# Attention with a spectral mix: the last sixteen modes regrouped by row transfers

## The chip, the cores and the metric

The kernel runs on one core of one Trainium2 chip. The metric is the device time of one execution in microseconds (us), lower is better. Of several runs the median is taken.

## The reference

The first half is a linear attention over 8 batches, 8 heads, 576 positions and 64 features per head. The second half mixes its result `x` (8 x 576 x 512) in the frequency domain: of the Fourier transform along the positions, the first 64 modes are multiplied by a complex 512 x 512 matrix each, transformed back and added, and a dense layer with a relu follows.

```python
X = np.fft.rfft(x, axis=1)
Xr, Xi = (np.real(X[:, :n_modes]), np.imag(X[:, :n_modes]))          # n_modes = 64
Yr = np.einsum('bmd,mde->bme', Xr, w_r) - np.einsum('bmd,mde->bme', Xi, w_i)
Yi = np.einsum('bmd,mde->bme', Xr, w_i) + np.einsum('bmd,mde->bme', Xi, w_r)
Y[:, :n_modes] = Yr + 1j * Yi
y = np.fft.irfft(Y, n=S, axis=1)
u = x + y
return (u + np.maximum(u @ w_ch, 0.0)).astype(np.float32)
```

## The kernel before

**The modes.** The 64 mode matrices come in 32 steps, `k` = 0 to 31. A step from k=8 on takes a group `gi` of eight modes (0 to 7) and 128 of the 512 input features, and loads two weight tiles, real (`wr`) and imaginary (`wi`), with one DMA each from the POOL queue (L162); `NW` = 3 steps may be in flight. `mode_mm` (L416) makes eight products with `wr` and eight with `wi` into one PSUM tile `psY`; each fills 32 of its 128 rows. For the last eight steps (k=24 to 31) the sum over the feature blocks is complete after the step: `mode_sum` (L444, VectorE) adds `psY` to the accumulator and leaves `yst`, which has a row for each mode, part (real or imaginary) and batch; the batch is the row's number modulo 8. Steps k=30 and k=31 are the groups gi=6 and gi=7, the last sixteen modes.

**From modes to batches.** The output needs the spectrum by batch: the tile `zy` has 128 rows (modes and parts) by [Z or Y, batch, 512], where Y is the spectrum and Z is Y times `w_ch`. `yst` is transposed on TensorE (L805), copied to `sY` by VectorE (L806), and for each pair of groups `by_batch` makes, in two halves h of four batches, Z (`mm_z`, L705) and Y itself (`mm_r`, a product with the identity, L711), 32 rows at a time, because a product takes the 32 columns of one batch from `sY`. The results lie in two PSUM tiles `psZY` (tags T0 and T1). For the first three pairs they are copied to `zy` by ScalarE (h=0) and VectorE (h=1), L718, a bit at a time, out of a list `copies` that `pieces` works off. For the last pair one batch of each half is copied in place (batches 0 and 4), and the whole of `psZY` is copied to `st` (L735), from which six DMAs of 64 KB, two on SP and four on POOL, move the other rows (L737).

**The work beside it.** `pieces` also runs the products of `x` with `w_ch` ahead: `flip_x` transposes a pair of tiles of `xs_all` (TensorE L654 into PSUM tag T3, VectorE copy `sT` L657), and `times_w` multiplies them (L665 into `psW`, tag T2, ScalarE copy `xw` L667). `reordered` (L692, `psX`, tags T0 and T1; copy L694) permutes rows of `xs_all`. Every PSUM tag has one buffer, so a tile waits until the tag's last tile has been read.

**The output units.** Twenty units, five for each pair of batches (b, b+4), in the order (b, b, b+4, b+4, both). A unit adds `xw` through an identity (`add_xw`, L753) and the transform of Z (`add_z`, L760) in a tile `psB`, relu by ScalarE (L762); `x` (`add_x`, L768) and the transform of Y (`spec`, L774) in `psA`, added by VectorE (L776). "Late" units add `x` on GpSimd (L780) instead. The result leaves by DMA from SP (L856). For unit 0 (`u0`), `add_xw` and `add_x` are run early, within k=31; its `psB` has tag T2 and its `psA` tag T3.

**Order.** All of this runs under a manual schedule: each engine runs its instructions in the order of the program text, and waits where data or a buffer is not ready. In step k=30 the end of the text is `times_w`; step k=31 begins with `add_xw(u0)`, then `mode_mm`, `mode_sum` in two halves, the transposes in two halves (T0, T1), `add_x(u0)`, `by_batch`.

Of the kernel before, what the change touches and what calls it, by code (L numbers as in the profile page):

```python
# [10 lines left out]
F32 = mybir.dt.float32  # L11
F32R = mybir.dt.float32r
BF16 = mybir.dt.bfloat16
I32 = mybir.dt.int32
ACT = mybir.ActivationFunctionType
ALU = mybir.AluOpType
# [4 lines left out]
DMODEL = 512  # L21
# [5 lines left out]
def kernel(  # L27
# [11 lines left out]
    nc = tc.nc  # L39
# [4 lines left out]
    psum = psum_cm.__enter__()  # L44
    pw = ctx.enter_context(tc.tile_pool(name="pw", bufs=3))

    ident_b = const.tile([128, 128], BF16, name="ident_b")
# [8 lines left out]
    Yacc = pers.tile([128, 8, DMODEL], F32, name="Yacc")  # L56
    wchb = pers.tile([128, 4, DMODEL], BF16, name="wchb")
# [54 lines left out]
    W = {}  # L112
# [274 lines left out]
                             start=(dc == 0), stop=(dc == 3))  # L387
        nc.scalar.copy(xw0[:, i, :], ps)

    def mode_mm(k, tag="yr"):  # L390
        g, gi = groups[k]
        XT = XTs[1 - g if k < 8 else g % 2]
        wt = W.pop(k)
        if gi < 0:
            psY = psum.tile([128, 2, DMODEL], F32, name="psY2", tag="pC", bufs=1)
            for par in range(2):
                for ri in range(2):
                    for j in range(4):
                        for x in range(2):
                            r = slice(64 * x, 64 * x + 64)  # L400
                            m = 16 * (-1 - gi) + 8 * x + 2 * j + par
                            c0 = (16, 0, 48, 32)[2 * ri + par]
                            nc.tensor.matmul(
                                psY[32 * j:32 * j + 32, x, :],
                                lhsT=XT[r, c0:c0 + 32, m],
                                rhs=wt[ri][r, 2 * j + par, :],
                                start=(par == 0 and ri == 0), stop=(par == 1 and ri == 1),
                            )
            return psY
        psY = psum.tile([128, DMODEL], F32, name="psY", tag=tag, bufs=1)  # L410
        for ri in range(2):
            for par in range(2):
                for j in range(4):
                    m = 8 * gi + 2 * j + par
                    c0 = (16, 0, 48, 32)[2 * ri + par]
                    nc.tensor.matmul(  # L416
                        psY[32 * j:32 * j + 32, :],
                        lhsT=XT[:, c0:c0 + 32, m],
                        rhs=wt[ri][:, 2 * j + par, :],
                        start=(par == 0 and ri == 0), stop=(par == 1 and ri == 1),  # L420
                    )
        return psY

    def mode_sum(k, psY, pb=None):
        g, gi = groups[k]
        if gi < 0:
            G = -1 - gi
            if g == 0:
                nc.vector.tensor_copy(Yacc[:, 2 * G:2 * G + 2, :], psY)
            else:  # L430
                nc.vector.tensor_tensor(
                    out=Yacc[:, 2 * G:2 * G + 2, :], in0=psY, in1=Yacc[:, 2 * G:2 * G + 2, :],
                    op=ALU.add)
        elif g < 3:
            nc.vector.tensor_tensor(  # L435
                out=Yacc[:, gi, :], in0=psY, in1=Yacc[:, gi, :], op=ALU.add)
        else:

            cuts = [0, DMODEL] if k < 31 else [0, DMODEL // 2, DMODEL]
            yst = []  # L440
            for a, b in zip(cuts, cuts[1:]):
                t = pb.tile([128, b - a], BF16, name="yst", tag="yst" if k < 31 else f"yst{a}",
                            bufs=2 if k < 31 else 1)
                nc.vector.tensor_tensor(out=t, in0=psY[:, a:b], in1=Yacc[:, gi, a:b], op=ALU.add)  # L444
                yst += [t[:, x:x + 128] for x in range(0, b - a, 128)]
            return yst


# [76 lines left out]
    psY = None  # L525
# [3 lines left out]
    with tc.manual_schedule():  # L529
# [25 lines left out]
        for n in range(N + 2):  # L555
# [9 lines left out]
            if psY is not None:  # L565
                mode_sum(k_out, psY)
                psY = None
# [54 lines left out]
            if k_out < K_IN_ATTN and n >= after[k_out] + 2:  # L622
                psY = mode_mm(k_out)
# [10 lines left out]
    pb = ctx.enter_context(tc.tile_pool(name="pb", bufs=2))  # L634

    psum = ctx.enter_context(tc.tile_pool(name="psumT", bufs=1, space=bass.MemoryType.PSUM))
# [4 lines left out]
    zy = pb.tile([128, 2, B_, DMODEL], BF16, name="zy", bufs=1)  # L641
    zall, yall = zy[:, 0], zy[:, 1]
# [5 lines left out]
    copies = []  # L648
# [11 lines left out]
    def times_w():  # L660
        i, sT = ahead.pop(0)
        ps = psum.tile([128, 2, DMODEL], F32, name="psW", tag="T2")
        for x in range(2):
            for dc in range(4):
                nc.tensor.matmul(ps[:, x, :], lhsT=sT[:, x, dc, :], rhs=wchb[:, dc, :],  # L665
                                 start=(dc == 0), stop=(dc == 3))
        nc.scalar.copy(xw[:, i - N_EARLY:i + 2 - N_EARLY, :], ps)  # L667
# [29 lines left out]
    def by_batch(sY, P):  # L697
        cols = [sY[:, dc].rearrange("p g c -> p (g c)") for dc in range(4)]

        ps = [psum.tile([128, 2, DMODEL], F32, name="psZY", tag=f"T{h}") for h in range(2)]  # L700

        def mm_z(h):
            for dc in range(4):
                for j in range(4):
                    nc.tensor.matmul(ps[h][32 * j:32 * j + 32, 0, :], lhsT=cols[dc][:, j + 4 * h::8],  # L705
                                     rhs=wchb[:, dc, :], start=(dc == 0), stop=(dc == 3))

        def mm_r(h):
            for dc in range(4):
                for j in range(4):  # L710
                    nc.tensor.matmul(  # L711
                        ps[h][32 * j:32 * j + 32, 1, dc * 128:(dc + 1) * 128],
                        lhsT=cols[dc][:, j + 4 * h::8], rhs=ident_b, start=True, stop=True)

        rows = slice(32 * P, 32 * P + 32)

        def copy(j, h, eng):
            eng(zy[rows, :, j + 4 * h, :], ps[h][32 * j:32 * j + 32])  # L718

        if P < 3:  # L720
            for h in range(2):
                mm_z(h)
                mm_r(h)
            copies.extend([lambda j=j: (copy(j, 0, nc.scalar.copy),
                                        copy(j, 1, nc.vector.tensor_copy)) for j in range(4)])
            return

        for h, eng in ((0, nc.scalar.copy), (1, nc.vector.tensor_copy)):  # L730
            mm_z(h)
            mm_r(h)
            copy(0, h, eng)
            st = pb.tile([128, 2, DMODEL], BF16, name=f"st{h}", bufs=1)
            eng(st, ps[h])  # L735
            for j in range(1, 4):
                (nc.sync if j == 1 else nc.gpsimd).dma_start(  # L737
                    zy[rows, :, j + 4 * h, :], st[32 * j:32 * j + 32])

    def parts(u):
# [21 lines left out]
    def add_x(u):  # L764
        u["psA"] = ps = psum.tile([128, 2, DMODEL], F32, name="psA", tag=u["tags"][1])
        if not u["late"]:
            for r, x, b, c, idn, ci in parts(u):
                nc.tensor.matmul(ps[r, x, :], lhsT=idn, rhs=xs_all[:, b * NCH + c, :],  # L768
                                 start=True, stop=False)
# [15 lines left out]
    with tc.manual_schedule():  # L785
        plan = {22: 3, 23: 3, 24: 2, 25: 2, 26: 2, 27: 1, 28: 2, 29: 1, 30: 1, 31: 0}
        while k_out < 32:
            k = k_out
            gi = groups[k][1]
            while k_in < min(k_out + NW, 32):  # L790
                weights(k_in)
                k_in += 1
            if k == 31:
                add_xw(u0)
            yst = mode_sum(k, mode_mm(k, "T3"), pb)
            k_out += 1
            if yst is not None:
                if ahead:
                    times_w()
                if gi % 2 == 0:  # L800
                    sY = pb.tile([128, 4, 2, 128], BF16, name="sY", tag="sY")
                for a, b, tag in ((0, 4, "T3"),) if k < 31 else ((0, 2, "T0"), (2, 4, "T1")):
                    pt = psum.tile([128, b - a, 128], BF16, name="ptY", tag=tag)
                    for dc in range(a, b):
                        nc.tensor.transpose(pt[:, dc - a, :], yst[dc], ident_b)  # L805
                    nc.vector.tensor_copy(sY[:, a:b, gi % 2, :], pt)  # L806
                if k == 31:
                    add_x(u0)
                if gi % 2 == 1:
                    by_batch(sY, gi // 2)  # L810
            pieces(plan[k])
            if k <= 24 or k % 2 == 0:
                assert not copies
                for tag in ("T0", "T1"):
                    if reorder:
                        reordered(tag)
            if k == 30:
                times_w()
        assert not todo and not ahead and not reorder and not copies

    units = []
# [65 lines left out]
```

## Time and profile before

| | before |
|---|---|
| median of 3 runs | 456.16 us (455.45 to 456.48) |
| profiled execution, first to last instruction (its span) | 456.7 us; the profile gives no other time of its own |
| TensorE busy | 301.7 us (66%) |
| VectorE busy | 292.0 us (64%) |
| ScalarE busy | 261.8 us (57%) |
| GpSimd busy | 198.8 us (44%) |
| DMA | 97.70 MB, 214 GB/s on average |
| mean granted TensorE clock | 0.883 of full speed |

A row of the profile's timeline has the start and duration in us, the engine (PE is TensorE, PEld its weight load, DVE VectorE, ACT ScalarE, POOL GpSimd, SP the sync engine), the line of the kernel, the operation, what it writes and reads, the shape, how many such instructions were merged, and in brackets how long the engine was idle before it and what ended that. The granted clock is the share of full speed at which TensorE may run. Busy shares are means over stages that differ: the weights stream in until shortly before the end, and the last 40 us are the output.

### The profile page before, as it was taken

How to read it: one execution, taken by the hardware profiler on the slowest of the kernel's cores; microseconds unless marked ns; L12 is line 12 of the kernel's file. 1: busy time of each engine (PE TensorE's matmuls, PEld its weight loads, DVE VectorE, ACT ScalarE, POOL GpSimd, SP SyncE). 2: the span in 40 equal slices, each digit the busy share in tenths (PEclk: the TensorE clock that was granted, in tenths of full speed). 3: DMA queues.
4: the chain of work that ended last, by engine and by line, in shares of the span. 5: the costliest groups of instructions: out<-in, count | busy, mean ns of one | idle time of the engine just before them, and what ended most of it. 6: DMA issues, size and time to landing. Idle time of an engine off the chain costs nothing.

```text
span 456.7 us, 11065 instructions
## 1 busy us (share of the span) xinstructions
PE 301.7 (66%) x4637; PEld 197.6 (43%) x4637; DVE 292.0 (64%) x418; ACT 261.8 (57%) x528; POOL 198.8 (44%) x251
## 2 busy tenths in 40 slices
PE   3476776833767677655555544755578878868993
PEld 2355565622555565544333432433344445433341
DVE  6578789844988779876666472776322273653873
ACT  4576887833686877865545452765334455644662
POOL 3956476445563256553435231443021212100993
PEclk9976899876886769998778595999999999998997
DMA  6999999999999999999999999999999999990697
GB/s 179 195 228 222 225 213 226 221 206 216 221 228 217 230 219 222 224 219 229 218 207 217 218 218 218 207 203 207 207 207 207 207 207 207 207 179 11 223 341 299
DMA packets 84417, 97.70 MB, mean 214 GB/s; under 512 B 3152, under 2 KB 77136, under 8 KB 84368
## 3 DMA queue, kind: packets, MB, share of 16 engines
q0 software_dynamic: 75728, 76.75, 101.1%
q1 hardware_dynamic: 8480, 20.19, 12.8%
q8 instruction: 36, 0.59, 0.5%
q14 instruction: 13, 0.11, 0.1%
q10 hardware_dynamic: 160, 0.07, 0.1%
HBM read 163.64 MB, written 9.44 MB: 379 GB/s over the span
## 4 chain that ended last, share of the span: by engine, by line
DMA 34%; issue 24%; DVE 17%; PE 11%; POOL 7%; ACT 3%; SPq 1%; DVEq 0%; POOLq 0%; ACTq 0%
DMA wi<-in_moe_w_i_dram 29%; DVE mkq L233 6%; DMA wr<-in_moe_w_r_dram 4%; DVE xs_all L336 2%; DVE nd L322 2%; DVE tB L315 2%; POOL vaug L270 2%; PE ptr L184 1%; PE psNB L305 1%; ACT AA L240 1%; PE kvz L286 1%; PE psB L753 1%; DVE of L776 1%; SPq L122 1%; POOL wr L162 1%
## 5 line engine op out<-in xcount | busy, mean ns | idle before, releaser
L270 POOL TENSOR_TENSOR vaug<-vn,ee 128x576 bf16<-128x576 f32 x64 | 72.7, 1155 | 63.3 <-ACT ee L255 50.2
L240 ACT ACTIVATE AA<-psT 128x1024 bf16<-128x1024 f32 x64 | 62.0, 1021 | 43.6 <-PE psT L208 43.1
L262 ACT ACTIVATE e<-mkq 64x4 f32<-64x4 f32 (+1 forms) x128 | 26.3, 206 | 61.5 <-DVE mkq L233 59.2
L244 ACT ACTIVATE AA<-psk 128x1024 bf16<-128x1024 f32 x64 | 61.4, 1010 | 0.0
L162 POOL DMA_DIRECT2D wr<-in_moe_w_r_dram x24 | 21.9, 912 | 86.6 <-PE psY L416 77.8
L416 PEld LDWEIGHTS <-XT 128*32 128x32 bf16 x384 | 17.1, 171 | 56.6 <-issue 46.4
L667 ACT CAST xw<-psW 128x1024 bf16<-128x1024 f32 x17 | 17.2, 1013 | 40.5 <-PE psW L665 34.6
L233 DVE TENSOR_REDUCE mkq<-psk 128x8 f32<-128x1024 f32 x32 | 38.8, 1213 | 0.7 <-PE psk L199 0.7
L233 DVE TENSOR_REDUCE mkq<-psq 128x8 f32<-128x1024 f32 x32 | 38.9, 1217 | 0.4 <-PE psq L199 0.4
L435 DVE TENSOR_TENSOR Yacc<-psY,Yacc 128x512 f32<-128x512 f32 x16 | 11.0, 689 | 42.5 <-PE psY L416 42.5
L416 PE MATMUL psY<-wi,XT 128*32 128x512 bf16 x192 | 18.0, 435 | 28.8 <-DMA wi<-in_moe_w_i_dram 28.8
L286 PE MATMUL kvz<-vaug,AA 64*128 64x65 bf16 x1152 | 29.2, 210 | 11.5 <-POOL vaug L275 9.8
L190 DVE COPY kT<-ptr 128x640 bf16<-128x640 bf16 x32 | 15.7, 492 | 32.5 <-PE ptr L184 32.5
L665 PE MATMUL psW<-wchb,sT 128*128 128x512 bf16 x136 | 33.5, 391 | 2.1 <-ACT xw L667 2.1
L315 DVE TENSOR_TENSOR tB<-psNB,e 128x650 f32<-128x650 f32 x32 | 26.7, 833 | 11.2 <-PE psNB L305 10.6
L305 PEld LDWEIGHTS <-AA 128*128 128x128 bf16 x640 | 29.0, 110 | 9.3 <-issue 8.9
L286 PEld LDWEIGHTS <-AA 64*128 64x128 bf16 x1152 | 25.1, 107 | 15.9 <-issue 11.8
L162 POOL DMA_DIRECT2D wi<-in_moe_w_i_dram x24 | 21.1, 880 | 23.8 <-PE psY L416 20.5
L322 DVE TENSOR_TENSOR nd<-psNA,tB 128x650 f32<-128x650 f32 x32 | 26.7, 835 | 4.1 <-DVE tB L315 0.5
L416 PE MATMUL psY<-wr,XT 128*32 128x512 bf16 x192 | 17.0, 424 | 18.0 <-DMA wr<-in_moe_w_r_dram 8.7
L336 DVE TENSOR_TENSOR xs_all<-nd,rden 128x640 bf16<-128x640 f32 x32 | 28.0, 874 | 1.1
L184 PE MATMUL ptr<-ident_b,k 128*128 128x128 bf16 x160 | 17.9, 257 | 14.8 <-DVE qT L190 12.6
(132 smaller groups left out, 705.4 us busy)
## 6 DMA issues: line engine op xcount, KB each, us to landing
wr<-in_moe_w_r_dram POOLq DMA_DIRECT2D x24, 1024.0 KB, 25.8
wi<-in_moe_w_i_dram POOLq DMA_DIRECT2D x24, 1024.0 KB, 29.4
wr<-in_moe_w_r_dram POOLq DMA_DIRECT2D x16, 512.0 KB, 15.9
wi<-in_moe_w_i_dram POOLq DMA_DIRECT2D x16, 512.0 KB, 19.6
out_dram<-of SPq DMA_DIRECT2D x16, 512.0 KB, 3.8
vn<-in_v_dram SPq DMA_DIRECT2D x24, 288.0 KB, 5.8
q<-in_q_dram POOLq DMA_DIRECT2D x12, 288.0 KB, 19.3
k<-in_k_dram POOLq DMA_DIRECT2D x12, 288.0 KB, 20.0
```

What stands on the lines that cost most here:

```text
L162: nc.gpsimd.dma_start(t, w[8 * gi:8 * gi + 8, g * 128:(g + 1) * 128, :].rearrange("m p e -> p m e"))
L233: nc.vector.tensor_reduce(out=o, in_=i, axis=AX.X, op=ALU.max, apply_absolute_value=True)
L240: nc.scalar.activation(AA[:, 0, ab, 0:1024].rearrange("f (x j p) -> f j x p", j=2, p=64), st["psT"].rearrange("f j (x p) -> f j x p", p=64 ...
L244: nc.scalar.activation(AA[:, 1, ab, 0:1024].rearrange("p (c j f) -> p j c f", c=4, j=2), st["psk"], ACT.Exp, scale=sc)
L270: nc.gpsimd.tensor_tensor(out=vaug[:, ab, :, 0:64], in0=st["v"], in1=ee[:, ab, :].unsqueeze(2).to_broadcast([128, 9, D_]), op=ALU.mult,)
L286: nc.tensor.matmul(kvz[:, hh, ab * 65:(ab + 1) * 65], lhsT=AA[r, 1, ab, 128 * j:128 * j + 128], rhs=vaug[r, ab, j, :], start=(j == 0), sto ...
L305: nc.tensor.matmul(p[:, hh, 65 * c:65 * c + 65], lhsT=AA[:, 0, ab, x:x + 128], rhs=kvzF[:, hh, ab * 65:(ab + 1) * 65], start=True, stop=True,)
L315: nc.vector.tensor_tensor(out=tB, in0=st["psNB"], in1=e2.unsqueeze(3).to_broadcast([128, 2, NCH, 65]), op=ALU.mult,)
L322: nc.vector.tensor_tensor(out=nd, in0=st["psNA"], in1=st["tB"], op=ALU.add)
L336: nc.vector.tensor_tensor(out=xo, in0=nd[:, :, :, 0:64], in1=rden.to_broadcast([128, 2, NCH, 64]), op=ALU.mult,)
L416: nc.tensor.matmul(psY[32 * j:32 * j + 32, :], lhsT=XT[:, c0:c0 + 32, m], rhs=wt[ri][:, 2 * j + par, :], start=(par == 0 and ri == 0), sto ...
L665: nc.tensor.matmul(ps[:, x, :], lhsT=sT[:, x, dc, :], rhs=wchb[:, dc, :], start=(dc == 0), stop=(dc == 3))
```

## The change

Groups gi=6 and gi=7 no longer go through `by_batch`. For each, `by_row` moves the rows of `yst` to `yall` by seven DMAs of 16 rows (16 KB), one for each batch from 1 to 7: batches 4 and 1 on SP, 5, 2, 6, 3, 7 on POOL. `z_of_group` makes Z of the group as one product of 128 rows (four matmuls of 128 x 512 into `psZ`: tag T3 for group 6, T1 for group 7), copies it half by ScalarE and half by VectorE to `z8`, and moves the rows by the same seven DMAs to `zall`. So there are 28 transfers of 16 KB where there were 6 of 64 KB. Batch 0 of both groups is made in place (`first_batch`, tag T0): four Z products and four identity products of 32 rows, copied to `zy` by ScalarE and VectorE. Batch 4, which was copied in place, comes by DMA.

In step k=31 the real products of `mode_mm` come first and lie in tag T1 (T3 before); then `times_w` (which was the end of step 30) and `add_x(u0)`, then the imaginary products, then `add_xw(u0)` (which was the first of the step). `yst` has one tile with three buffers.

```diff
-    def mode_mm(k, tag="yr"):
+    def mode_mm(k, tag="yr", ris=(0, 1), psY=None):
...
-        psY = psum.tile([128, DMODEL], F32, name="psY", tag=tag, bufs=1)
-        for ri in range(2):
+        if psY is None:
+            psY = psum.tile([128, DMODEL], F32, name="psY", tag=tag, bufs=1)
+        for ri in ris:
...
+            yst = pb.tile([128, DMODEL], BF16, name="yst", tag="yst", bufs=3)
             cuts = [0, DMODEL] if k < 31 else [0, DMODEL // 2, DMODEL]
...
-        for h, eng in ((0, nc.scalar.copy), (1, nc.vector.tensor_copy)):
+        for h in range(2):
             mm_z(h)
             mm_r(h)
-            copy(0, h, eng)
-            st = pb.tile([128, 2, DMODEL], BF16, name=f"st{h}", bufs=1)
-            eng(st, ps[h])
-            for j in range(1, 4):
-                (nc.sync if j == 1 else nc.gpsimd).dma_start(
-                    zy[rows, :, j + 4 * h, :], st[32 * j:32 * j + 32])
-
+        copies.extend([lambda j=j: (copy(j, 0, nc.scalar.copy),
+                                    copy(j, 1, nc.vector.tensor_copy)) for j in range(4)])
+
+    def by_row(all_b, t, gi):
+        for b in (4, 1, 5, 2, 6, 3, 7):
+            (nc.sync if b in (4, 1) else nc.gpsimd).dma_start(
+                all_b[16 * gi:16 * gi + 16, b, :], t[b::8, :])
+
+    def first_batch(sY):
+        cols = [sY[:, dc].rearrange("p g c -> p (g c)")[:, 0::8] for dc in range(4)]
+        ps = psum.tile([128, 2, DMODEL], F32, name="psZY", tag="T0")
+        r = slice(96, 128)
+        for dc in range(4):
+            nc.tensor.matmul(ps[r, 0, :], lhsT=cols[dc], rhs=wchb[:, dc, :],
+                             start=(dc == 0), stop=(dc == 3))
+        for dc in range(4):
+            nc.tensor.matmul(ps[r, 1, dc * 128:(dc + 1) * 128], lhsT=cols[dc], rhs=ident_b,
+                             start=True, stop=True)
+        nc.scalar.copy(zall[r, 0, :], ps[r, 0, :])
+        nc.vector.tensor_copy(yall[r, 0, :], ps[r, 1, :])
+
+    def z_of_group(sY, gi):
+        ps = psum.tile([128, DMODEL], F32, name="psZ", tag="T3" if gi == 6 else "T1")
+        for dc in range(4):
+            nc.tensor.matmul(ps, lhsT=sY[:, dc, gi % 2, :], rhs=wchb[:, dc, :],
+                             start=(dc == 0), stop=(dc == 3))
+        z = pb.tile([128, DMODEL], BF16, name="z8", tag="z8")
+        nc.scalar.copy(z[:, 0:256], ps[:, 0:256])
+        nc.vector.tensor_copy(z[:, 256:512], ps[:, 256:512])
+        by_row(zall, z, gi)
...
-            if k == 31:
+            if k < 31:
+                psY = mode_mm(k, "T3")
+            else:
+                psY = mode_mm(k, "T1", ris=(0,))
+                times_w()
+                add_x(u0)
+                mode_mm(k, ris=(1,), psY=psY)
                 add_xw(u0)
-            yst = mode_sum(k, mode_mm(k, "T3"), pb)
+            yst = mode_sum(k, psY, pb)
             k_out += 1
             if yst is not None:
+                if gi >= 6:
+                    by_row(yall, yst, gi)
                 if ahead:
                     times_w()
...
-                if k == 31:
-                    add_x(u0)
-                if gi % 2 == 1:
+                if gi == 7:
+                    first_batch(sY)
+                if gi >= 6:
+                    z_of_group(sY, gi)
+                elif gi % 2 == 1:
                     by_batch(sY, gi // 2)
             pieces(plan[k])
...
-            if k == 30:
-                times_w()
```

More of the change, by code (lines that the diff above doesn't have):

```diff
@@ L388, in times_w_early @@
         nc.scalar.copy(xw0[:, i, :], ps)
-    def mode_mm(k, tag="yr"):
+    def mode_mm(k, tag="yr", ris=(0, 1), psY=None):
         g, gi = groups[k]
         XT = XTs[1 - g if k < 8 else g % 2]
-        wt = W.pop(k)
+        wt = W[k]
         if gi < 0:
@@ L437, in mode_sum @@
         else:
+            yst = pb.tile([128, DMODEL], BF16, name="yst", tag="yst", bufs=3)
             cuts = [0, DMODEL] if k < 31 else [0, DMODEL // 2, DMODEL]
-            yst = []
             for a, b in zip(cuts, cuts[1:]):
[L442 to L445, printed above, removed]
+                nc.vector.tensor_tensor(out=yst[:, a:b], in0=psY[:, a:b], in1=Yacc[:, gi, a:b],
+                                        op=ALU.add)
             return yst
@@ L718, in copy @@
             eng(zy[rows, :, j + 4 * h, :], ps[h][32 * j:32 * j + 32])
[L720 to L726, printed above, removed]
-        for h, eng in ((0, nc.scalar.copy), (1, nc.vector.tensor_copy)):
+        for h in range(2):
             mm_z(h)
             mm_r(h)
-            copy(0, h, eng)
-            st = pb.tile([128, 2, DMODEL], BF16, name=f"st{h}", bufs=1)
-            eng(st, ps[h])
-            for j in range(1, 4):
-                (nc.sync if j == 1 else nc.gpsimd).dma_start(
-                    zy[rows, :, j + 4 * h, :], st[32 * j:32 * j + 32])
+        copies.extend([lambda j=j: (copy(j, 0, nc.scalar.copy),
[25 more added lines that the diff above has]
+        by_row(zall, z, gi)
     def parts(u):
@@ L804 @@
                     for dc in range(a, b):
-                        nc.tensor.transpose(pt[:, dc - a, :], yst[dc], ident_b)
+                        nc.tensor.transpose(pt[:, dc - a, :], yst[:, dc * 128:(dc + 1) * 128],
+                                            ident_b)
                     nc.vector.tensor_copy(sY[:, a:b, gi % 2, :], pt)
-                if k == 31:
-                    add_x(u0)
-                if gi % 2 == 1:
+                if gi == 7:
[3 more added lines that the diff above has]
+                elif gi % 2 == 1:
                     by_batch(sY, gi // 2)
```

## The prediction

> **What bounds the kernel now.** I read the page first, then the timeline from 400 us to the end, the granted clock in steps of 1 us from 404 to 421, the landing of the last weights, and the DMA issues after 395 us. Until the weights of the last group (k=31) have landed the kernel waits for the weight stream: the page's chain gives 29% of the span to the imaginary weights. Behind that landing there is a serial piece, and then the output units, which TensorE, GpSimd and the output DMA all but fill. The change lies in the piece between.
>
> The last weight issue and its landing: 388.44 + 26.0 = 414.4 us (the issue of k=30, at 380.99, is the one that took 23.6: its products start on the landing).
>
> ```profile
> 388.44 0.88 POOL L162 DMA_DIRECT2D wi<-in_moe_w_i_dram  x1
> ...
> DMA to landing us min/median/max: 23.6/24.8/26.0
> ```
>
> The timeline from k=30 to the first outputs (start, duration, what; in brackets idle time and who ended it):
>
> ```profile
> 407.42 0.42 DVE L806 COPY sY<-ptY 128x512 bf16<-128x512 bf16 x1 [1.36 <-PE ptY L805]
> 407.90 0.61 PE L654 MATMUL pt<-ident_b,xs_all 128*128 128x128 bf16 x8 [0.52 <-DVE sY L806]
> 408.54 0.69 DVE L657 COPY sT<-pt 128x1024 bf16<-128x1024 bf16 x1 [0.70 <-PE pt L654]
> 409.26 2.46 DVE L718 CAST zy<-psZY 32x1024 bf16<-32x1024 f32 x2
> 410.29 0.59 PE L692 MATMUL psX<-xs_all,ident_p 128*128 128x512 bf16 x2 [1.79 <-ACT zy L718]
> 410.72 3.22 PE L665 MATMUL psW<-wchb,sT 128*128 128x512 bf16 x8
> 413.98 1.01 ACT L667 CAST xw<-psW 128x1024 bf16<-128x1024 f32 x1 [2.05 <-PE psW L665]
> 415.04 0.59 PE L753 MATMUL psB<-xw,ident_p 128*128 128x512 bf16 x2 [1.10 <-ACT xw L667]
> 415.56 0.69 PE L416 MATMUL psY<-wr,XT 128*32 128x512 bf16 x8
> 416.08 0.60 PE L416 MATMUL psY<-wi,XT 128*32 128x512 bf16 x8
> 417.55 0.62 DVE L806 COPY sY<-ptY 128x256 bf16<-128x256 bf16 x2
> 421.93 1.23 DVE L735 CAST st<-psZY 128x1024 bf16<-128x1024 f32 x1
> 423.07 2.35 DVE L776 TENSOR_TENSOR of<-psA,of 128x1024 f32<-128x1024 f32 x2
> 425.50 8.40 POOL L780 TENSOR_TENSOR of<-of,xs_all 128x1024 f32<-128x1024 f32 x4 [0.98 <-DVE of L776]
> 425.77 2.52 DVE L776 TENSOR_TENSOR of<-psA,of 128x1024 f32<-128x1024 f32 x2 [0.36 <-ACT of L762]
> ```
>
> Two facts decide. The imaginary products of k=31 start at 416.08, 1.6 us after their weights: they stand behind psW, its ACT copy and psB. And psW took 3.22 us here, where the same eight products take 1.89 to 1.90 at 392.54 and 405.26. The windows say why (PE, PEld, DVE, ACT, POOL, then clock, DMA share, GB/s):
>
> ```profile
> 409.00:410.00 1.00, 0.00 (x0) 0.00 (x0) 0.97 (x2) 0.99 (x2) 0.00 (x0) 1.00 0.64 108
> 411.00:412.00 1.00, 1.00 (x4) 0.34 (x3) 0.73 (x1) 0.93 (x1) 0.00 (x0) 0.56 0.38 62
> 412.00:413.00 1.00, 1.00 (x4) 0.42 (x3) 0.00 (x0) 0.00 (x0) 0.00 (x0) 0.50 0.17 28
> ```
>
> After a thin stretch (of the 3.4 us before 411.1 TensorE was busy 1.4: the transposes' 0.61 and 0.8 from 410.29) the clock is half for 3.4 us; that stretch was then dense and full speed returned at 414.5.
>
> **The change, part by part.** Times are those of this execution, 456.66 us from first to last instruction, 0.50 above the median of 456.16.
>
> *k=30.* Group 6 gets its Z product between the sY copy (ends 407.84) and flip_x, in the same PSUM tag T3. Four products 128x512: 1.03 us, as the four psX products at 378.16. ACT copies 256 columns: 1024 take 1.01 and 512 take 0.60 (relu into Yacc), so 0.40 by the slope. DVE's half waits for ACT's (the built program's wait list has it): 0.38, as one half of the two yst adds (0.76). With hand-overs of 0.05: 1.95. flip_x waits for that DVE copy to free T3, so its transposes go from 407.90 to 409.86, sT to 410.50, the two DVE copies out of psZY from 409.26–411.72 to 411.22–413.68. psX, which waits for ACT's copies, goes from 410.29 to about 411.5. The row transfers of group 6 (5 on POOL and 2 on SP for each of Y and Z) queue behind the last weights and delay nothing that is awaited; POOL has no other work then. They add 0.22 MB to a stream of 207 GB/s: at most 1.1 us on the landing, which has more than that to spare below.
>
> *k=31, real products first.* psY now lies in T1, and T1 holds psZY of the previous pair until DVE's second copy ends, 413.68. So the real products start at 413.74, not early. Behind them in TensorE's order: times_w (8 products), add_x (2), then the imaginary products. At full clock 0.43 + 1.72 + 0.43 from 413.74 gives 416.3. At half clock a 512-column product takes 0.43 (the weight loads of psW stand at 411.60, 412.03, 412.45, 412.88): 0.86 + 3.43 + 0.43 to 0.86. What was done while the weights came is now done after them.
>
> *Which clock?* From 408.97 (end of the Z products) to 413.74 TensorE has only the transposes (0.61) and psX (0.59) in 4.8 us. A stretch like 407.7–411.1 holds 1.6 of 3.4, and 411.1–414.5 some 1.4: as thin as the 1.4 that brought half clock before. I take half clock until 417.9, then full: real products to 414.6, times_w to 418.03, add_x to 418.46, imaginary products done 419.06 against 416.68. add_xw waits for ACT's copy of psW (418.2 + 1.01), ends 419.7, and the transposes behind it start there, 0.2 later than yst allows. The second sY copy ends at 420.67 against 418.17: 2.50 late.
>
> The Trainium skill ("TensorE: Matmul & The Clock Gate", Part 1) has it that the clock halves after an idle window of about 3.4 us, and asks for no idle gaps above that; by that the full clock would hold here, since the longest gap is 1.7 us, and the time is that of the first rival below. The trace does not agree: half clock came at 411.1 with no gap above 1.8 us (408.51 to 410.29). The same page's Part 4 says that transposes don't count as busy, which would make the stretch thinner still; no run here shows that alone.
>
> *After sY.* Before: 64 products (418.20–420.64), then on ACT 1.00 + 1.01 and on DVE 1.22 + 1.23 (copy, st); unit 0's add at 423.07, unit 2's at 425.77, that is 4.90 and 7.60 after sY. Now the first batch's four Z products (0.86, the first two already on the first half of sY) and four small ones (0.22) end at 421.65. ACT copies 32x512 (0.60), DVE after it 0.67 (half of 1.22 and a fixed part). The group's Z product ends 422.5, ACT's half of it 422.95, then relu of unit 0 to 424.03, its add at 424.07; unit 1's add 425.65–426.88. Unit 2 (batch 4) used to be copied in place and now needs the z8 transfer: issued on SP behind z8's DVE half, 423.45, and 2.1 to land (the zy<-st issues on SP): 425.55. Then two Z products 0.60, relu 1.02, and the add at 427.3, or 6.6 after sY against 7.6. Gain 0.97. SP's four transfers stand ahead of the first output but cost it nothing (it is ready at 425.3). POOL issues five more, 423.45 + 5 x 0.56 = 426.3, before its first add, which needs unit 1 at 426.9 (425.50 before, 1.4 late). From there the units run as before: TensorE is busy 4.9 to 5.0 of 5 us, POOL idles 0.8 us between 425.50 and 449.45.
>
> Sum: 2.50 – 0.97 = 1.5 by unit 2, 1.4 by POOL. I take 1.45: 458.1 in a profiled execution, 457.6 in the median. The boundary of the clock's stretch can lie elsewhere: half clock ending 417.1 gives 420.2 for sY (+1.0), ending 419.2 gives 421.15 (+2.0). So 457.2 to 458.1 for this case.
>
> **The rivals.**
> 1. *Full clock through.* Real products to 414.2, times_w to 415.9, imaginary products done 416.95, add_xw from 417.2, sY 418.6: 0.43 late, minus 0.97, is –0.55: 455.6, not slower. For: several stretches about 0.5 busy kept full clock (the late slices of the page show 9 throughout). Against: the row at 411. It decides if the stretch before 414.5 counts as busier than the one before 411.1.
> 2. *The imaginary products do start on the landing* (414.5) at full clock, because DVE's copies leave T1 some 2 us earlier than I have it and times_w is through by then: done 415.1, sY 416.7, –1.5 – 0.97 = –2.5: 453.7. For: that is how the order is written. Against: T1's copies stand behind sT, sT behind the Z product.
> 3. *POOL decides.* If a row transfer costs POOL the 0.88 of a weight issue and not 0.56, five from 423.45 end at 427.85, 1.0 after unit 1's add; POOL has no slack, so +2.5: 458.6. It decides above 0.69 each. Against: the 64 KB issues took 0.54 to 0.56, and these are smaller.
>
> **How the numbers follow.** Forecast 0.60, rivals 0.20, 0.08 and 0.12. 0.2% (0.9 us) is about what a measurement of this kernel can tell. Faster: rival 2 and a fifth of rival 1 (a tail gain above mine), 0.12. Same: the rest of rival 1, and 0.08 for the low end of the forecast, whose 457.2 is next to the bound: 0.24. Slower: 0.64. The range runs from rival 1 to the long half clock with a little of rival 3, 455.5 to 458.9; the forecast's own is 457.0 to 458.4.
>
> **What would show it.** In the changed profile: the real products of k=31 starting near 413.7, released by DVE's zy copy; psW behind them taking 3.2 to 3.4; imaginary products starting near 418.4, over 3 us after the landing; unit 0's add some 3.4 after sY; unit 2's Z products released by a DMA. Wrong if the real products start before 412, if the clock stays 1.00 from 411 to 418, or if POOL's first add waits for POOL itself.

## The result

The changed kernel is slower: 459.41 us in the median of 22 runs (458.06 to 461.21), against 456.98 for the kernel before, run beside it 22 times (455.39 to 460.27). The ratio is 1.005, with a 95% interval of 1.0033 to 1.0066, that is +2.4 us. The forecast was 457.6 with a range to 458.9: the direction came, the size did not, and the time lies above the range. Of the 1.8 us between forecast and time, 0.8 is the base (a median of 456.16 in three runs, 456.98 in 22); the other 1.0 is the change itself, which was forecast at +1.45. The profiled execution has a span of 458.7 us at a mean clock of 0.867, and the time measured for it is 460.56. In all 22 runs the time is 1.73 to 1.86 us longer than the span (on record to 0.1 us), a figure that was not known when the forecast was made, and that matters below.

The last weights of the changed kernel are issued at 390.5 and land 22.4 us later, at 412.9:

```profile
L162 POOL DMA_DIRECT2D wi<-in_moe_w_i_dram x1: 881/881/881, 390.5 to 390.5; - x1
...
DMA to landing us min/median/max: 18.2/20.3/22.4
```

The timeline of the changed kernel from step 30 to the first units (start, duration, engine, line, operation, what it writes and reads; in brackets the idle time and who ended it):

```profile
408.42 0.42 DVE L827 COPY sY<-ptY 128x512 bf16<-128x512 bf16 x1 [0.49 <-PE ptY L825]
410.37 0.42 DVE L750 CAST z<-psZ 128x256 bf16<-128x256 f32 x1 [1.53 <-ACT z L749]
410.85 0.61 PE L653 MATMUL pt<-ident_b,xs_all 128*128 128x128 bf16 x8 [0.92 <-DVE z L750]
412.20 2.46 DVE L717 CAST zy<-psZY 32x1024 bf16<-32x1024 f32 x2
412.44 0.59 PE L691 MATMUL psX<-xs_all,ident_p 128*128 128x512 bf16 x2 [0.98 <-ACT zy L717]
414.72 0.69 PE L417 MATMUL psY<-wr,XT 128*32 128x512 bf16 x8 [1.69 <-DVE zy L717]
415.34 3.46 PE L664 MATMUL psW<-wchb,sT 128*128 128x512 bf16 x8
419.29 0.69 PE L417 MATMUL psY<-wi,XT 128*32 128x512 bf16 x8
420.83 0.62 DVE L827 COPY sY<-ptY 128x256 bf16<-128x256 bf16 x2
424.35 1.12 SPq L727 DMA_DIRECT2D zy<-z  x2
424.61 2.39 POOL L727 DMA_DIRECT2D zy<-z  x5 [1.16 <-DVE z L750]
424.98 1.22 DVE L788 TENSOR_TENSOR of<-psA,of 128x1024 f32<-128x1024 f32 x1 [0.66 <-ACT of L774]
427.74 2.13 POOL L792 TENSOR_TENSOR of<-of,xs_all 128x1024 f32<-128x1024 f32 x1 [0.74 <-DVE of L788]
```

The real products stand behind a wait of 1.69 us for VectorE's copies out of T1. The imaginary products, whose weights had landed at 412.9, start 6.4 us later, behind real products, `times_w` and `add_x`. And psW takes 3.46 us instead of 1.89. The granted clock of the same kernel (PE, PEld, DVE, ACT, POOL busy, then clock, DMA share, GB/s) shows TensorE all but idle just before, then half clock:

```profile
413.00:414.00 1.00, 0.03 (x1) 0.09 (x1) 0.99 (x2) 0.94 (x1) 0.82 (x2) 1.00 0.01 2
...
416.00:417.00 1.00, 1.00 (x4) 0.41 (x3) 0.00 (x0) 0.00 (x0) 0.00 (x0) 0.50 0.00 0
417.00:418.00 1.00, 1.00 (x4) 0.33 (x3) 0.00 (x0) 0.00 (x0) 0.00 (x0) 0.50 0.00 0
```

All this is the walk that was forecast. What is not so plain is where the further microsecond of the result comes from. Two executions are laid beside each other here from a common point, because the time at which step 30 is reached scatters: VectorE's sY copy of step 30 (the first row above, 407.42 in the profile before) starts anywhere from 405.33 to 408.92 in the fourteen executions that were profiled. Counted from that copy, in us, with the experiments told of below:

| execution | psW start, duration | imaginary weights landed | imaginary products start | second sY copy ends | unit 2's add | end of span |
|---|---|---|---|---|---|---|
| before (the profile shown) | 3.30, 3.22 | 6.98 | 8.66 | 10.75 | 18.35 | 49.2 |
| before, profiled again | 2.87, 1.89 | 5.11 | 6.89 | 8.97 | 16.57 | 47.4 |
| before, a third profile | 3.31, 1.89 | 7.31 | 7.35 | 9.51 | 17.11 | 48.0 |
| before, filled | 3.19, 1.89 | 7.60 | 7.64 | 9.81 | 17.42 | 48.3 |
| after | 6.92, 3.46 | 4.48 | 10.87 | 13.03 | 19.35 | 50.3 |
| after, profiled again | 6.93, 3.46 | 6.60 | 10.88 | 13.05 | 19.37 | 50.3 |
| after, filled | 6.94, 1.90 | 7.05 | 9.20 | 11.37 | 17.69 | 48.6 |
| after, `times_w` first | 4.45, 1.89 | 5.75 | 7.21 | 9.30 | 15.62 | 46.6 |
| after, Z of group 6 late | 4.99, 1.90 | 7.12 | 7.25 | 9.42 | 15.74 | 46.7 |
| both of these | 3.30, 1.89 | 7.53 | 7.57 | 9.73 | 16.05 | 47.0 |
| regrouping alone | 4.45, 1.89 | 7.96 | 8.47 | 10.56 | 17.19 | 48.2 |
| new order alone | 5.39, 2.74 | 6.31 | 8.49 | 10.65 | 17.96 | 48.8 |

From the same point, the changed kernel ends 1.0 us later than the profile before that the forecast walked along, but 2.3 to 2.9 later than the other two executions of the kernel before. The first profile of before was a late one in this very piece.

### The profile page after: what moved, and what is told of

Read it like the earlier page. It is cut to its first block, busy times and chain, and to the rows that moved or that the text cites. A ratio compares the mean times of both kernels' runs of the same rounds, so it can differ in the third digit from the quotient of the medians.

```text
span 458.7 us, 10996 instructions
## 1 busy us (share of the span) xinstructions
PE 311.5 (68%) x4589; PEld 200.7 (44%) x4589; DVE 293.8 (64%) x419; ACT 261.3 (57%) x529; POOL 206.3 (45%) x267
## 4 chain that ended last, share of the span: by engine, by line
DMA 34%; PE 24%; DVE 23%; ACT 6%; issue 5%; POOL 5%; SPq 1%; DVEq 0%; ACTq 0%; POOLq 0%
DMA wi<-in_moe_w_i_dram 18%; DMA k<-in_k_dram 6%; PE psW L664 5%; DVE mkq L233 5%; DMA wr<-in_moe_w_r_dram 5%; DMA q<-in_q_dram 4%; DVE xs_all L336 3%; DVE zy L717 3%; DVE nd L322 3%; PE psY L417 3%; DVE tB L315 2%; ACT AA L240 2%; POOL vaug L270 2%; PE pt L653 2%; PE psB L765 1%
## 5 line engine op out<-in xcount | busy, mean ns | idle before, releaser
L417 PE MATMUL psY<-wi,XT 128*32 128x512 bf16 x192 | 19.2, 466 | 24.5 <-DMA wi<-in_moe_w_i_dram 24.5
L417 PE MATMUL psY<-wr,XT 128*32 128x512 bf16 x192 | 18.2, 453 | 18.4 <-DMA wr<-in_moe_w_r_dram 7.9
L208 PE MATMUL psT<-qT,w 64*128 64x512 bf16 x64 | 15.5, 475 | 20.9 <-DVE mkq L233 20.9
```

The source lines that it names most:

```text
L417: nc.tensor.matmul(psY[32 * j:32 * j + 32, :], lhsT=XT[:, c0:c0 + 32, m], rhs=wt[ri][:, 2 * j + par, :], start=(par == 0 and ri == 0), sto ...
```

## The experiments

Three theories stood against each other. Theory 1 (the clock): the thin stretch ahead of step 31 brings half clock on `times_w`, and the kernel before has that in some executions only. Theory 2 (the order): at any clock, Z of group 6 ahead of flip_x holds T1 and psW back, and `times_w` behind the real products holds the imaginary ones. Theory 3: the loss arises before 400 us, where the two profiles were already 2.0 us apart.

### Both kernels again

No edit.

> The kernel before, profiled once more. All theories: no change in time (ratio 1.000). Theory 1 (clock: in the changed kernel the products of x with w_ch in step 31 nearly always fall into half clock, in the kernel before only in some executions): this second profile may well show the eight products psW of step 30 in 1.9 us at full clock, not 3.2, and the imaginary products then start on their weights' landing. Theory 2 (order: the changed kernel does after the landing what was done before it, and the clock adds nothing): the imaginary products again start over 1 us after the landing. Theory 3 (the loss arises before 400 us, as the 2.0 us between the two profiles do): the flip of step 29 stands near 402 again, 2 us ahead of the changed kernel's.

> The changed kernel, profiled once more: ratio to before 1.005. Theory 1: psW of step 31 again takes 3.2 to 3.5 us. Theory 2: it may take 1.9 and the time is the same. Theory 3: the flip of step 29 stands near 404 again.

Measured: before 457.0 us, ratio 1.0009 (0.9987 to 1.0031); after 459.2, ratio 1.0049 (1.003 to 1.0067). The second profile of the kernel before shows its end piece at full clock:

```profile
410.62 1.89 PE L665 MATMUL psW<-wchb,sT 128*128 128x512 bf16 x8
413.61 0.59 PE L753 MATMUL psB<-xw,ident_p 128*128 128x512 bf16 x2 [1.10 <-ACT xw L667]
414.64 0.61 PE L416 MATMUL psY<-wi,XT 128*32 128x512 bf16 x8
```

and the second one of the changed kernel has the half clock again:

```profile
413.92 0.69 PE L417 MATMUL psY<-wr,XT 128*32 128x512 bf16 x8 [1.69 <-DVE zy L717]
414.54 3.46 PE L664 MATMUL psW<-wchb,sT 128*128 128x512 bf16 x8
```

These two executions start step 30 within 0.14 us of each other (407.75 and 407.61), and their spans are 455.12 and 457.90. So the loss, 2.8 us here, lies behind step 30, and theory 3 falls for this pair. Scatter as large as the 2.0 us by which the first two profiles differ at 400 us meets the kernel before alone: its three profiles reach the sY copy at 407.42, 407.75 and 405.48. The clock differs between them long before that. Here is 325 to 330 us of two of them (columns as in the windows above, the second profile first and then the third):

```profile
325.00:330.00 5.00, 3.16 (x13) 1.61 (x13) 1.29 (x3) 0.96 (x2) 0.00 (x0) 0.66 1.24 207
```

```profile
325.00:330.00 5.00, 3.04 (x21) 1.57 (x22) 0.68 (x2) 1.50 (x3) 0.00 (x0) 1.00 1.24 207
```

The same kernel has a mean clock of 0.66 there once, and full speed once. That this makes the scatter is likely but not shown.

### Filling the thin stretch

Products that nobody reads are put where TensorE waits, so that the stretch isn't thin. Both kernels get:

```diff
+    def fill(n):
+        ps = psum.tile([128, 2, DMODEL], F32, name="psFill", tag="T2")
+        for i in range(n):
+            nc.tensor.matmul(ps[:, i % 2, :], lhsT=ident_b, rhs=xs_all[:, 0, :],
+                             start=True, stop=True)
```

In the kernel before, `fill(7)` stands between flip_x and psX of step 30. In the changed kernel `fill(4)` stands there, and `fill(7)` between psX and the real products of step 31.

> The kernel before with seven products 128x512 more in step 30, between flip_x and psX, where TensorE idles; nobody reads their result. They keep TensorE busy, so the half clock should not come. Theory 1: psW 1.9 us, and 0.3 to 0.9 us faster than before (1.5 us in the executions that had half clock, none in the others), 456.1 to 456.7 on the median of 457.0. Theories 2 and 3: no change.

> The changed kernel with eleven products 128x512 more, four between flip_x and psX of step 30 and seven between psX and the real products of step 31, where TensorE idles; nobody reads their result. Theory 1: psW of step 31 takes 1.9 us and not 3.5, and the kernel is 1.3 to 1.7 us faster than the changed one: about 458.0, or 1.002 of before. Theories 2 and 3: 459.4, no change.

Measured: before filled 456.5 us, ratio 0.9982 (0.9966 to 0.9998); after filled 457.89, ratio 1.0011 (0.9988 to 1.0034). The timeline of the filled changed kernel:

```profile
411.64 1.67 PE L757 MATMUL psFill<-xs_all,ident_b 128*128 128x512 bf16 x7
413.49 0.69 PE L417 MATMUL psY<-wr,XT 128*32 128x512 bf16 x8 [0.18 <-DMA zy<-z]
414.12 1.90 PE L664 MATMUL psW<-wchb,sT 128*128 128x512 bf16 x8
416.38 0.68 PE L417 MATMUL psY<-wi,XT 128*32 128x512 bf16 x8
```

Real products and psW start where they did (6.31 and 6.94 after the sY copy, against 6.31 and 6.93), but psW is at full clock, and the imaginary products start 1.68 earlier. By the ratios the fill gives the changed kernel back 0.38% (1.7 us), and the kernel before 0.18% (0.8 us). So theory 1 holds: work without any use makes both faster (the kernel before only just clear of no change), and the change loses more to the clock, 0.9 us net. What is left between the filled kernels is 0.29% or 1.3 us, at full clock in the one profile of each: theory 2 has its share too. The intervals are about 0.2% wide to each side, so the split into 0.9 and 1.3 is rough.

### times_w ahead of the real products

```diff
-                psY = mode_mm(k, "T1", ris=(0,))
                 times_w()
                 add_x(u0)
-                mode_mm(k, ris=(1,), psY=psY)
+                psY = mode_mm(k, "T1")
                 add_xw(u0)
```

> The changed kernel, but times_w and add_x stand ahead of the real products of step 31, which follow with the imaginary ones in one go. Theories 1 and 2 (order): times_w no longer stands behind the wait for PSUM tag T1, it starts when sT is there (some 2.5 us after the group 6 Z copy), and the imaginary products start within 0.7 us of the real ones; with the gain behind sY (1.0 to 1.4) the time is 455.6 to 456.5, 0.997 to 0.999 of before. Theory 3: 459.4, no change.

Measured: 456.5 us, ratio 0.9983 (0.9964 to 1.0003). The timeline:

```profile
413.37 1.89 PE L664 MATMUL psW<-wchb,sT 128*128 128x512 bf16 x8
415.62 0.69 PE L417 MATMUL psY<-wr,XT 128*32 128x512 bf16 x8
```

Now psW fills the wait for T1 instead of standing behind it: it starts 4.45 after the sY copy (6.92 in the changed kernel) and at full clock, and the real products start 6.70 after it, 0.4 later than in the changed kernel. Giving up "real products first" takes back the whole loss, 0.66% by the ratios.

### Z of group 6 behind the pieces of step 30

```diff
-                if gi >= 6:
+                if gi == 7:
                     z_of_group(sY, gi)
...
             pieces(plan[k])
+            if k == 30:
+                z_of_group(sY, gi)
```

> The changed kernel, but the Z product of group 6 follows flip_x and its copies instead of preceding them. Theories 1 and 2: T1 is free 1.95 us earlier, and so the real products of step 31 start 1.9 us earlier against step 30's yst; 457.0 to 457.5 if psW still falls into half clock, 455.7 if not. Theory 3: no change from 459.4.

Measured: 455.36 us, ratio 0.997 (0.9953 to 0.9988): faster than both kernels. The timeline:

```profile
410.92 0.70 PE L417 MATMUL psY<-wr,XT 128*32 128x512 bf16 x8 [1.04 <-DVE zy L717]
411.55 1.90 PE L664 MATMUL psW<-wchb,sT 128*128 128x512 bf16 x8
413.81 0.68 PE L417 MATMUL psY<-wi,XT 128*32 128x512 bf16 x8
```

The real products start 4.36 after the sY copy instead of 6.30: that is, to 0.01, the 1.95 that the forecast gave to Z ahead of flip_x. They still wait for T1 (1.04), but no half clock follows, and the imaginary products start 0.13 behind their landing.

### Each half of the change alone

Regrouping alone is the changed kernel with the order of step 31 as it was (`add_xw(u0)` first, both products of the mode in T3, then `add_x(u0)`, and `times_w` at the end of step 30). New order alone is the kernel before with

```diff
-            if k == 31:
+            if k < 31:
+                psY = mode_mm(k, "T3")
+            else:
+                psY = mode_mm(k, "T1", ris=(0,))
+                times_w()
+                add_x(u0)
+                mode_mm(k, ris=(1,), psY=psY)
                 add_xw(u0)
...
-            if k == 30:
-                times_w()
```

> Only the regrouping (row transfers, Z of a group, batch 0 in place), in the order of before: times_w at the end of step 30, add_xw first in step 31, real and imaginary products together in T3, add_x after the transposes. Theories 1 and 2: psW and the imaginary products 1.2 us later than before (the Z product of group 6 ahead of flip_x), 1.0 to 1.4 gained after sY: 456.5 to 457.5, within 0.1% of before; the loss belongs to the reordering. Theory 3: near 459.4.

> Only the new order of step 31 (real products in T1, times_w, add_x, imaginary products, add_xw), with by_batch and the transfers of st as before. Theories 1 and 2: T1 is free at DVE's second zy copy (0.05 us before psW starts in the kernel before plus some 1 us), so psW stands 1.5 us later than before but the imaginary products follow it at once: 456.5 to 458.0, nothing gained after sY. Theory 3: no change from before, 457.0.

Measured: regrouping alone 457.71 us, ratio 1.0009 (0.9993 to 1.0025), within the 0.1% that was expected though 0.2 us above the times; new order alone 458.21, ratio 1.0038 (1.0019 to 1.0057), also 0.2 us above what was expected. Their sum, 0.47%, is the whole change's 0.49 to 0.5%. Regrouping alone shows a loss and a gain of about a microsecond each: psW starts 4.45 after the sY copy (2.87 to 3.31 before), and unit 2's add stands 6.63 behind the second sY copy (7.60 before). The new order alone is the dearer half, and its profile has half clock (psW 2.74) where that of the regrouping alone has none.

### The new order filled

The new order alone, with `fill(5)` between flip_x and psX of step 30 and `fill(5)` between psX and the real products.

> Only the new order of step 31, with ten products 128x512 more that nobody reads: five between flip_x and psX, five between psX and the real products. Without them the profile had half clock from 410.9 to 414.3, real products 1.1 and psW 2.7 us. Theory 1: both at full clock, 1.0 to 1.3 us faster than without, 457.0 to 457.3, no longer slower than before. Theory 2: 458.2 as without.

Measured: 455.59 us, ratio 0.9991 (0.9973 to 1.001), lower than expected. The window from 410 to 414 us, the new order alone first, then filled:

```profile
410.00:414.00 4.00, 2.69 (x13) 0.96 (x13) 1.44 (x2) 1.01 (x1) 0.00 (x0) 0.61 0.28 46
```

```profile
410.00:414.00 4.00, 4.00 (x29) 1.47 (x26) 0.50 (x2) 1.01 (x1) 0.00 (x0) 1.00 0.25 41
```

Without the fill TensorE is idle a third of the time and gets a clock of 0.61. With it, it is busy throughout at full speed, and the imaginary products start 0.04 after their landing (412.77 and 412.73). Counted from the sY copy the second window lies 1.8 us later than the first; at the same place, 408.17 to 412.17, the filled version is busy for 3.96 us, also at full speed. The fill gives back 0.47%, more than the 0.38% that the new order lost, and the filled kernel before (0.9982) is only 0.09% ahead, within the noise. So without Z of group 6 ahead, no loss of the new order is left once the clock is full.

### Z late, filled

The version with Z of group 6 late, with `fill(3)` ahead of that Z and `fill(4)` ahead of the real products.

> The changed kernel with the Z product of group 6 behind flip_x, and with seven products 128x512 more that nobody reads: three between flip_x and the Z product, four between psX and the real products of step 31. Its companion without them had psW at full clock in its profile, so theory 1 (clock) leaves little: only the executions that fell into half clock gain. 454.8 to 455.4, 0.995 to 0.997 of before. If the clock never mattered (theory 2): 455.4 as without them, or later by what the seven delay.

Measured: 455.99 us, ratio 0.9983 (0.9965 to 1.0001). This missed what theory 1 gave: the filled version isn't faster than the unfilled one (0.997), and the intervals overlap. It fits the other expectation, no gain from the fill. Its profile explains why there was little to gain: the imaginary products start 0.04 after the landing (413.73 and 413.69), where the unfilled version had 0.13. Where products already start on their landing, a fill has nothing to win.

### Both mendings together

Z of group 6 late and `times_w` ahead of the real products, both edits as above.

> The changed kernel with the Z product of group 6 behind flip_x and with times_w and add_x ahead of the real products of step 31. With the Z product late alone the imaginary products started 0.13 us after their weights had landed (413.81 against 413.68), so the weights set the end there. Theories 1 and 2: nothing more to gain from the order, 455.1 to 455.7, 0.996 to 0.998 of before. If the wait for T1 ahead of times_w was what still cost: 454.5 or less.

> The kernel before, a third profile, one look: does the half clock stand on the psW of step 30? Theory 1 wants it in a minority of the executions (one of two so far).

Measured: 454.8 us, ratio 0.9959 (0.9941 to 0.9976), 1.9 us faster than the kernel before and the lowest of all that were run, though its interval overlaps that of Z late alone. It lies between the two expectations (455.1 or more, 454.5 or less) and decides for neither. The third profiled execution of the kernel before took 455.27, at full clock in this piece:

```profile
408.79 1.89 PE L665 MATMUL psW<-wchb,sT 128*128 128x512 bf16 x8
```

The timeline of the mended version:

```profile
409.27 1.89 PE L664 MATMUL psW<-wchb,sT 128*128 128x512 bf16 x8
411.52 0.69 PE L417 MATMUL psY<-wr,XT 128*32 128x512 bf16 x8
413.54 0.69 PE L417 MATMUL psY<-wi,XT 128*32 128x512 bf16 x8 [1.33 <-DMA wi<-in_moe_w_i_dram]
```

psW starts 3.30 after the sY copy, as early as before. The real products are done ahead of the landing, and the imaginary ones wait for the weights and for nothing else. What is left of the change is what it brings behind sY: unit 2's add 6.32 after it instead of 7.60.

## Why the prediction was right and wrong

**The step that failed is the one from the profiled execution to the median.** The forecast took the walk's 456.66 as 0.50 above the median of 456.16, and so gave 458.1 less 0.50. But 456.66 was a span. A time is 1.73 to 1.86 us longer than its span in the runs of the changed kernel, and in the later runs of the kernel before too, which puts the time of that execution near 458.5, some 1.5 above the median of 456.98. With 1.8 added in place of 0.50 taken off, the same walk gives 459.9 for one execution, and the median came at 459.41. That execution was late for a reason that lay in the very piece of the walk: psW at half clock, 3.22 us, which one of three profiles of the kernel before has and two have not. The change was charged for a half clock that the base was taken to have always. In fact the base has it sometimes, and the change had it in both profiles. The gap between 456.66 and the three times shown, which were from 455.45 to 456.48, could have warned: a span above all the times that go with it, though a time holds the span, says that the execution isn't typical.

**The walk itself held.** From the sY copy of step 30, against the profile that it was made along:

- *Z ahead of flip_x:* 1.95 forecast. Flip_x's transposes start 2.43 after the sY copy against 0.48, that is 1.95.
- *The wait for T1:* the real products start 6.30 after the sY copy, forecast 6.32 (413.74 less 407.42), and VectorE's zy copy releases them, after 1.69 us of idle TensorE.
- *Half clock on `times_w`:* 3.46, forecast as 3.43. The place is right too: the granted clock is half from 415.51 for 3.41 us, some 7.1 to 10.5 after the sY copy; forecast until 10.5. That the place came to 0.1 us has luck in it, as told below.
- *The second sY copy:* 2.50 late forecast, 2.28 measured (13.03 against 10.75).
- *Behind sY:* a gain of 0.97 forecast, 1.28 measured (6.32 against 7.60 to unit 2's add). The mis-sized term is the wait of unit 2 for its row transfer, the first of the two on SP: it was to land 2.1 us after its issue, as the 64 KB ones did, and landed after 1.7 (issued at 424.35). Unit 2's products with it start at 426.08, just behind the landing and hardly later than TensorE would have come to them; they lead to its add by way of the relu. Unit 0's add came 3.53 after sY, forecast 3.4.
- *Sum:* +1.45 forecast, +1.0 measured against that profile (50.28 against 49.24 from the sY copy to the end); 0.2 of the difference lies at the second sY copy, 0.3 behind it. Against the two other executions of the kernel before it is +2.3 and +2.9, and +2.4 in the medians.

**Rival 1** (full clock through, –0.55) had the right size against the profile that was walked: the filled changed kernel ends 48.6 after the sY copy, 0.6 less than that profile. But by the medians it is 0.1% above the kernel before, not clear of no change. Its mistake is that of the forecast: it let the change have full clock and the base not. **Rival 2** (imaginary products on the landing) came only in versions that give up a part of the change. It was priced at –2.5; the version with both mendings is 1.9 faster than the kernel before (0.9959). That supports the reason given against it: in the change as made, T1's copies stand in the way. **Rival 3** (POOL decides) fell: 0.48 for a transfer, below the 0.69 from which it would decide, and POOL's first add waits for unit 1's add and not for its own transfers.

**On the clock,** the reasoning from the row at 411 held: no gap of TensorE in the stretch before 415.51 is longer than 1.69 us, and half clock came. The Trainium skill ("TensorE: Matmul & The Clock Gate", Part 1) puts it behind an idle window of about 3.4 us; the trace doesn't agree. That products put into those shorter gaps removed it points to the sum of the gaps, not to one alone.

The traces show more than was read from them so far. Half clock came here for 3.41 us, right behind a stretch of 3.41 us in which TensorE was busy for 1.43 us (before), 1.39 (the changed kernel, either profile to 0.01) or 1.20 (new order alone). Laying such stretches end to end from there, the least busy one that was followed by full clock behind the sY copy had 1.62 (before, third profile). The boundary isn't sharp: 1.65 brought half clock once, in step 30 of the version with `times_w` first. So the place of the stretch goes with what the kernel before gets: it began 0.28 us after the sY copy in the profile that was walked, 0.58 in the third (1.62 busy) and 0.71 in the second (2.06). In the two profiles of the changed kernel stretches began at 0.26 and 0.28, as in the profile that was walked, and the one behind which half clock came was the next; that they lay alike is the luck in its place. Moving a stretch of 3.41 us in steps of 0.1 over one profile each, TensorE is busy for 1.45 us or less, the side on which half clock came, at 12 of 34 places in the kernel before, at 25 in the changed kernel, at 27 with the new order alone, and at none with Z of group 6 late, where the fill had nothing to win.

What stays open: whether the kernel before has the half clock in a third of its executions or in fewer or more, since only three were profiled and the 14 profiles don't spread evenly over the 34 places; and what moves the half-clock stretches between 308 and 330 us from one execution to the next.

## What to carry to other kernels

Before a walk along a profile is turned into a time, ask whether that execution is a typical one in the piece that is walked: a span already above the measured times says no, and a stretch at half clock in it may be there by chance. Work that was done while data came (here `times_w`) should stay in that wait; what is put ahead of it because its data are there gains nothing if its buffer comes free last, and the idle TensorE may then run the next dense work at half speed. Where new work goes ahead of a copy that frees a shared PSUM tag, try it behind that copy: here this one move turned 0.5% slower into 0.3% faster.

## What was not expected of the hardware

- Products that nobody reads made a kernel faster: eleven of 128x512, seven of them in the wait for T1, gave the changed kernel 0.38% by the ratios. The half-clock stretches lasted 3.41 us in every execution in which they hit this piece, and psW at half clock took 3.46 us for 1.89. They followed stretches of the same length in which TensorE was busy for 1.20 to 1.43 us, with no gap above 1.8 us.
- Three executions of the kernel before reached the sY copy of step 30 at 405.48, 407.42 and 407.75 us. Half-clock stretches fall differently in them: 0.66 and 1.00 was the mean clock from 325 to 330 us in two. That the one causes the other is not shown.
- Transfers of 16 KB cost POOL 0.48 us each to issue, where those of 64 KB took 0.54 to 0.56. There were 28 in place of 6, and no cost of them was seen: the version with both mendings has all 28 and the lowest time.
